# Masks copied by ScalarE, U's products in one group a batch, and small changes of loads, warm-ups and slots

## The chip, the cores and the metric

The kernel runs on one core of one Trainium2 chip. A core has five engines that work side by side: TensorE (PE) multiplies matrices, VectorE (DVE) and ScalarE (ACT) work on elements in the on-chip memory (SBUF) and in the accumulators (PSUM), GpSimd (POOL) works on SBUF, and SyncE (SP) issues transfers. Each engine runs its own list of instructions in order and waits on semaphores of the others. The metric is the device time of one execution in microseconds (us).

## What is computed

Inputs are q, k, v of shape (8, 8, 576, 64), U (576, 32), V (32, 576), w_ch1 (512, 2048) and w_ch2 (2048, 512), all float32. The reference is attention with two kinds of masks, followed by a mixing over the sequence and by an MLP:

```python
rel = pos[:, None] - pos[None, :]
mask_local = (rel >= 0) & (rel < 32)
mask_strided = (rel >= 0) & (pos[None, :] % 32 == pos[:, None] % 32)
# heads 0..3 local, heads 4..7 strided
scores = np.where(masks[None], q @ k.T / 8, -1000000000.0)
attn = np.exp(scores - scores.max(-1))
x = (attn / (attn.sum(-1) + 1e-09)) @ v        # (8, 8, 576, 64), as (8, 576, 512) below
h = x.T @ U @ V
u = x + h.T
out = u + np.maximum(u @ w_ch1, 0.0) @ w_ch2
```

## The kernel before

**The MLP.** The 8 × 576 rows are cut into nine blocks of 512: one for each batch, and a last one (the tail block) with the last 64 rows of all batches. For each block, `gemm1` and `gemm2` run over 16 slices of 128 hidden columns. float32 values are split in a high and a low part: `split` makes uh (ACT, L639) and ul (DVE, L640) of a block, `gemm1` does 12 products of 512 columns into a PSUM tile ph (L648), makes gh = relu(ph) on ACT (L652) and the rest gl on DVE (L653), and `gemm2` does 12 products into the block's accumulators acc (L665): two with gh and one with gl for each of four row groups. `gemm2` runs one slice behind `gemm1`. In the names below gl(w0) is the gl of a block's first slice, gl(w13) that of its fourteenth, ph(w10) the product tile of its eleventh. At the end of a block, `finish` adds acc to the rows on DVE (L672) and stores them. Weights of the first seven slices keep names (w0a, w0b and so on, a for the first layer and b for the second), the others are called w.

**The attention of the following batch** runs beside the MLP. For each batch it has two pairs of local heads (`local_pairs`): scores on PE (L346) on top of a mask that PE writes into the accumulator by a product with the identity (`scores`, L340), maximum and difference on DVE (L356, L357), exp on ACT, transposes on PE (L368), a copy on ACT (L371), the products with v (L381) and the normalising on DVE. All of these use one PSUM tile, px. The four strided heads of batches 2 to 7 (`strided_heads`) take no PE: POOL multiplies (L442 for the scores, L470 for the outputs) and DVE reduces (L444, L472), with softmax steps on DVE and ACT in between (L453 to L461). Reductions run one piece behind products: score row i has one piece up to i = 8 and two from i = 9 on (9 keys and the rest), an output row one piece up to i = 8 and two halves from i = 9 on. The buffers of POOL's pieces come from a group of five that the local pairs and the mixing use too (`att`). Batches 0 and 1 have all their heads done ahead of the MLP, with PE, by `first_attention`.

**The mixing.** `mix_t` multiplies a batch's rows with U in two halves of 256 columns (L514 and, for the last 64 rows, L518), adds the four parts on DVE (L525) and splits the result (L527 to L529); `mix_u` and `mix_tail` multiply it with V (L537, L546) and add it (L539, L552). `transposes` turns the rows (L619) and stores and loads them again as raw.

**What sets the order.** The program is written as a loop over slots, two for each slice. `advance` takes as many steps of the next batch's attention as A_EARLY or A_LATE say for that slot (first slot, last slot, number of steps), `strided_upto` paces the strided heads by S0 and S1, and `issue_after` keeps an instruction behind another. A scheduler then lists the instructions of each engine in the order in which they become ready in its own model of the program's timing, so that a moved slot can change the order on every engine.

**The start.** Masks, an identity in bf16 (both in masks_sb) and one in float32 are loaded on POOL's queue (`far_dma`); ACT's queue (`od_dma`) loads other things. Ahead of the first and of the second group of scores, `scores` runs 8 products of zeros (WARM).

Of the kernel before, what the change touches and what calls it, by code (L numbers as in the profile page):

```python
# [17 lines left out]
NSP = 2  # L18
N_EARLY = 20
N_LATE = 48  # L20
N_STRIDED = 66
# [16 lines left out]
def fused_kernel(ctx, tc, pairs, strided, U, V, w_in, masks, eye, out):  # L38
    nc = tc.nc
    B, S, DM = out.shape  # L40
    D = 64
# [50 lines left out]
    def psx1():  # L92
        return psx2()[:, 0, :]
# [237 lines left out]

    def scores(kT, qT, mask):

        sp = psx2()
        done = marks.setdefault("scores", [])
# [3 lines left out]
        for hh in range(2):  # L339
            nc.tensor.matmul(sp[:, hh, 0:320], ident_b, mask, start=True, stop=False, skip_group_check=True)  # L340
        for c in range(NCH):
            t, c4 = c // 4, c % 4
            k0 = max(0, 32 * c - 32)
            x0 = 64 * t + (0 if c else 32)
            for hh, rows in enumerate(halves):
                last = nc.tensor.matmul(sp[32 * c4:32 * c4 + 32, hh, x0:64 * t + 64], qT[rows, 32 * c:32 * c + 32],  # L346
                                        kT[rows, k0:32 * c + 32], start=False, stop=True, skip_group_check=True,
                                        tile_position=(64 * hh, 32 * c4))
# [25 lines left out]
    def outputs(PT, vt):  # L374

        op = psx2()
        for c in range(NCH):
            t, c4 = c // 4, c % 4
            for o4 in (c4,) if t < 4 else (c4, c4 + 2):
                for hh, rows in enumerate(halves):  # L380
                    last = nc.tensor.matmul(op[32 * o4:32 * o4 + 32, hh, (D + 1) * t:(D + 1) * t + D + 1],  # L381
                                            PT[rows, 32 * c:32 * c + 32], vt[rows, c], start=True, stop=True,
                                            skip_group_check=True, tile_position=(64 * hh, 32 * o4))
        marks.setdefault("PV", []).append(last.ins)
        return op[:, :, 0:5 * (D + 1)].rearrange("p h (t x) -> p h t x", x=D + 1)
# [15 lines left out]
    def local_pairs(b):  # L401
# [100 lines left out]

    def mix_t(b, half):

        xg, xt = x_tiles(b)
        tb = 64 * (b % 2)
        cs = slice(256 * half, 256 * half + 256)
        ps_a = psx1()[:, 0:256]
        if b not in tsts:
            tsts[b] = ap_.tile([96, DM], F32R, name="tst")  # L510
        tst = tsts[b]
        with tc.issue_after(marks["acc"][2 + half]) if b < NSP else nullcontext():
            for j in range(4):
                nc.tensor.matmul(ps_a[32 * j:32 * j + 32, :], U_sb[:, j, :], xg[:, j, cs], start=True, stop=False,  # L514
                                 skip_group_check=True, tile_position=(0, 32 * j))
        for j in range(4):
            part = slice(64 * j, 64 * j + 64)
            nc.tensor.matmul(ps_a[32 * j:32 * j + 32, part], U_sb[tb:tb + 64, 4, :],  # L518
                             xt[tb:tb + 64, 256 * half + 64 * j:256 * half + 64 * j + 64], start=False, stop=True,
                             skip_group_check=True, tile_position=(tb, 32 * j))  # L520
        yield
        ta = att([32, 256], "ta")
        nc.scalar.copy(out=ta, in_=ps_a[0:32, :])  # L523
        for j in range(1, 4):
            nc.vector.tensor_tensor(out=ta, in0=ps_a[32 * j:32 * j + 32, :], in1=ta, op=ALU.add)  # L525
# [44 lines left out]
    def first_attention():  # L570
# [73 lines left out]
    def gemm1(fc, dcs=range(NDC)):  # L644
        ph = ps_h.tile([128, 512], F32, name="ph")
        for dc in dcs:
            for i, (part, ut) in enumerate(((0, uh), (0, ul), (1, uh))):
                nc.tensor.matmul(ph, w_parts[fc, 0][:, part, 128 * dc:128 * dc + 128], ut[:, dc, :],  # L648
                                 start=(dc == dcs[0] and i == 0), stop=(dc == dcs[-1] and i == 2))
        gh = mp.tile([128, 512], F32R, name="gh", bufs=2)  # L650
# [177 lines left out]
```

## Time and profile before

| | us |
|---|---|
| three runs | 1476.99, 928.8, 930.89 |
| median | 930.89 |
| the profiled execution | 928.37 |
| its span | 926.1 |

The profile shows one execution. Its span is the time from the first to the last recorded work; 2.3 us lie around it. By the page PE is busy for 97% of the span, DVE for 59%, POOL for 37% and ACT for 26%. The mean granted clock of PE is 0.991 of full speed. Three views are used below. The timeline lists an engine's instructions with start and duration, neighbours of one kind grouped (x4 is four of them), and in brackets the idle time ahead of them with what ended it. The table by stretch gives busy times. The list of waits gives, for an engine and a line, whom it waited for: total, number, longest. Matmuls are pipelined: their durations overlap, so a matmul's price is the distance from start to start.

### The profile page before, as it was taken

The numbers are of one execution on the slowest core, as the hardware profiler recorded it, in microseconds if no ns is written. First come the engines' busy times: TensorE is split into PE (matmuls) and PEld (weight loads), VectorE is DVE, ScalarE is ACT, GpSimd is POOL, SyncE is SP. The second block draws the span as 40 slices with busy tenths as digits, with TensorE's granted clock in tenths as the row PEclk, the third lists the DMA queues.
The fourth block names the chain that finished last, engine by engine and source line by source line (L and its number), as shares of the span: only waits on it lengthen the run. The fifth ranks groups of instructions, "written<-read, shape, count | busy, mean of one in ns | idle before, by whom it ended". The sixth has DMA issues, their size and how long they took to land.

```text
span 926.1 us, 16819 instructions
## 1 busy us (share of the span) xinstructions
PE 902.6 (97%) x6997; PEld 718.0 (78%) x6998; DVE 548.6 (59%) x895; ACT 244.2 (26%) x478; POOL 338.4 (37%) x378
## 2 busy tenths in 40 slices
PE   7899989999999999999999999999999999999997
PEld 4667767777887788778877787778877888888885
DVE  4579996665886588658765786667863341122111
ACT  3457522142123312331224121422142111121110
POOL 1223493343853393429433764356530000000000
PEclk9899999999999999999999999999999999999999
DMA  9869313201230125011500141014200230001001
GB/s 352 299 205 357 117 54 107 73 2 52 76 145 2 52 55 178 1 52 33 181 8 18 50 168 50 1 53 148 73 1 1 57 120 17 1 1 46 0 1 46
DMA packets 39036, 75.29 MB, mean 81 GB/s; under 512 B 6464, under 2 KB 22864, under 8 KB 37040
## 3 DMA queue, kind: packets, MB, share of 16 engines
q1 hardware_dynamic: 27312, 66.87, 20.7%
q10 hardware_dynamic: 10560, 4.73, 2.0%
q0 software_dynamic: 1088, 2.62, 0.8%
q8 instruction: 55, 0.90, 0.4%
q14 instruction: 21, 0.17, 0.1%
HBM read 54.14 MB, written 11.67 MB: 71 GB/s over the span
## 4 chain that ended last, share of the span: by engine, by line
PE 84%; DVE 4%; DMA 2%; POOL 1%; issue 1%; ACT 0%; SPq 0%; DVEq 0%; ACTq 0%; POOLq 0%
PE acc L665 40%; PE ph L648 39%; PE px L381 1%; DMA w<-in_w_dram 1%; PE px L346 1%; DVE cv L132 1%; DVE s_st L444 1%; PE px L368 1%; PE px L514 1%; DMA od<-x 1%; PE px L537 1%; DMA st<-in_strided_dram 1%; DVE w L206 1%; POOL tmp L442 1%; DVE gl L653 0%
## 5 line engine op out<-in xcount | busy, mean ns | idle before, releaser
L653 DVE SCALAR_TENSOR_TENSOR gl<-ph,gh 128x512 fp32r<-128x512 f32 x144 | 98.9, 688 | 230.1 <-ACT gh L652 229.4
L648 PE MATMUL ph<-uh,w 128*128 128x512 f32 x648 | 215.9, 394 | 0.0
L652 ACT ACTIVATE gh<-ph 128x512 fp32r<-128x512 f32 x144 | 86.2, 599 | 476.9 <-PE ph L648 400.8
L470 POOL TENSOR_TENSOR tmp<-st,s_st 128x448 f32<-128x448 f32 (+7 forms) x162 | 137.3, 876 | 190.8 <-DVE st L472 106.8
L442 POOL TENSOR_TENSOR tmp<-st 128x576 f32<-128x576 f32 (+6 forms) x162 | 175.0, 1121 | 76.5 <-DMA st<-in_strided_dram 66.6
L665 PE MATMUL acc<-w,gh 128*128 128x512 f32 x648 | 196.8, 391 | 0.0
L648 PEld LDWEIGHTS ph<-uh,w 128*128 128x128 f32 x648 | 121.9, 189 | 26.8
L665 PEld LDWEIGHTS acc<-w,gh 128*128 128x128 f32 x648 | 121.3, 188 | 25.6
L472 DVE TENSOR_REDUCE st<-tmp 128x64 f32<-128x64 f32 (+8 forms) x162 | 136.3, 878 | 7.8 <-POOL tmp L470 7.0
L648 PE MATMUL ph<-ul,w 128*128 128x512 f32 x324 | 126.8, 391 | 0.0
L665 PE MATMUL acc<-w,gl 128*128 128x512 f32 x324 | 121.6, 392 | 4.1 <-DVE gl L653 4.1
L444 DVE TENSOR_REDUCE s_st<-tmp 128x9 f32<-128x576 f32 (+6 forms) x162 | 87.2, 563 | 17.5 <-POOL tmp L442 16.7
L665 PEld LDWEIGHTS acc<-w,gl 128*128 128x128 f32 x324 | 61.0, 188 | 18.4 <-DVE gl L653 5.2
L648 PEld LDWEIGHTS ph<-ul,w 128*128 128x128 f32 x324 | 61.1, 189 | 12.6
L487 ACT COPY xg<-st 32x256 f32<-32x256 f32 x96 | 38.8, 404 | 9.1 <-DVE st L472 7.7
L525 DVE TENSOR_TENSOR ta<-px,ta 32x256 f32<-32x256 f32 x42 | 17.6, 420 | 36.5 <-ACT ta L523 35.6
L672 DVE TENSOR_TENSOR xg<-acc,xg 128x512 f32<-128x512 f32 x36 | 22.9, 682 | 13.4 <-PE acc L665 13.4
L539 DVE TENSOR_TENSOR xg<-px,xg 128x512 f32<-128x512 f32 x28 | 18.0, 684 | 11.9 <-PE px L537 11.9
L648 PE MATMUL ph<-uh,w6a 128*128 128x512 f32 x72 | 24.3, 398 | 0.0
L640 DVE TENSOR_TENSOR ul<-raw,uh 128x512 fp32r<-128x512 f32 x32 | 21.1, 682 | 5.3 <-ACT uh L639 5.3
L648 PE MATMUL ph<-uh,w1a 128*128 128x512 f32 x72 | 23.9, 391 | 0.0
L648 PE MATMUL ph<-uh,w2a 128*128 128x512 f32 x72 | 23.9, 391 | 0.0
(265 smaller groups left out, 1252.9 us busy)
## 6 DMA issues: line engine op xcount, KB each, us to landing
w<-in_w_dram SPq DMA_DIRECT2D x9, 1024.0 KB, 13.3
out_dram<-xg SPq DMA_DIRECT2D x32, 256.0 KB, 2.1
v<-in_pairs_dram SPq DMA_DIRECT2D x12, 585.0 KB, 5.1
st<-in_strided_dram SPq DMA_DIRECT2D x6, 1152.0 KB, 5.4
qk<-in_pairs_dram SPq DMA_DIRECT2D x12, 576.0 KB, 5.1
late<-in_pairs_dram SPq DMA_DIRECT2D x8, 585.0 KB, 8.3
late<-in_pairs_dram SPq DMA_DIRECT2D x8, 576.0 KB, 8.1
raw<-bt SPq DMA_DIRECT2D x128, 32.0 KB, 1.9
```

The lines of the kernel that those rows point to most:

```text
L442: nc.gpsimd.tensor_tensor(out=tmp[:, 0:n], in0=sk[:, j0:j0 + n], in1=sq[:, i:i + 1].broadcast_to([128, n, D]), op=ALU.mult)
L444: late.append(lambda tmp=tmp, n=n, i=i, j0=j0: nc.vector.tensor_reduce(out=s_st[:, i, j0:j0 + n], in_=tmp[:, 0:n], axis=AX.X, op=ALU.add))
L470: nc.gpsimd.tensor_tensor(out=tv, in0=sv[:, 0:i + 1, d0:d0 + step], in1=s_st[:, i, 0:i + 1].broadcast_to([128, i + 1, step]), op=ALU.mult)
L472: late.append(lambda tv=tv, i=i, d0=d0, step=step: nc.vector.tensor_reduce(out=o_st[:, i, d0:d0 + step], in_=tv.rearrange("p j d -> p d j" ...
L487: nc.scalar.copy(out=xg[32 * i4:32 * i4 + 32, :, cs], in_=o_st[rows, i4:16:4, :])
L539: nc.vector.tensor_tensor(out=xg[:, t + s, :], in0=pv[:, s, :], in1=xg[:, t + s, :], op=ALU.add)
L640: nc.vector.tensor_tensor(out=lo, in0=raw[:, :, :, dc, :], in1=hi.bitcast(F32), op=ALU.subtract)
L648: nc.tensor.matmul(ph, w_parts[fc, 0][:, part, 128 * dc:128 * dc + 128], ut[:, dc, :], start=(dc == dcs[0] and i == 0), stop=(dc == dcs[-1 ...
L652: marks.setdefault("gh", []).append(nc.scalar.activation(out=gh, in_=ph, func=AF.Relu).ins)
L653: low = nc.vector.scalar_tensor_tensor(out=gl, in0=ph, scalar=0.0, in1=gh.bitcast(F32), op0=ALU.max, op1=ALU.subtract)
L665: last = nc.tensor.matmul(accs[n][s // 2][:, s % 2, :], gt[:, cs], w_parts[fc, 1][:, part, :], start=(fc == 0 and i == 0 and n > 0), stop= ...
L672: nc.vector.tensor_tensor(out=ot, in0=accs[n][s // 2][:, s % 2, :], in1=ot, op=ALU.add)
```

## The change

It has six parts.

- **Masks.** In batches 2 to 7 the mask of a pair is written into px by one ACT copy (`masked`, new) and no longer by two products on PE; the scores then accumulate onto it, and they are issued behind the latest product of gemm1.
- **Outputs.** In `outputs`, only the products of the first of five column groups start a sum afresh; the others add, and are kept behind the first.
- **Mixing.** `mix_t` does all 512 columns at once and stands behind the strided copies; before, its first half stood ahead of them.
- **Loads.** Masks and the identity are loaded on ACT's queue.
- **Warm-ups.** The second group of scores has 3 products of zeros, the first keeps 8.
- **Slots.** A_EARLY has 17 steps for 20, A_LATE has 47 for 48 and begins at slot 3 for 1.

```diff
-N_EARLY = 20
-N_LATE = 48
+N_EARLY = 17
+N_LATE = 47
-A_LATE = (1, 28, N_LATE)
+A_LATE = (3, 28, N_LATE)
-WARM = {0: 8, 1: 8}
+WARM = {0: 8, 1: 3}
...
+    def masked():
+        sp = psx2()
+        nc.scalar.copy(out=sp[:, :, 0:320], in_=mask_l.broadcast_to([128, 320, 2]).rearrange("p x h -> p h x"))
+        return sp
+
+    def scores(kT, qT, mask, sp=None):
+        if sp is None:
+            sp = psx2()
+            with_mask(sp, mask)
...
     def outputs(PT, vt):
         op = psx2()
+        first = None
         for c in range(NCH):
             t, c4 = c // 4, c % 4
+            with tc.issue_after(first) if t else nullcontext():
...
-                                            PT[rows, 32 * c:32 * c + 32], vt[rows, c], start=True, stop=True,
+                                                PT[rows, 32 * c:32 * c + 32], vt[rows, c], start=t == 0, stop=True,
...
-            sp = scores(kT, qT, mask_l)
+            sp = masked()
+            yield
+            with tc.issue_after(marks["ph"][-1]):
+                sp = scores(kT, qT, mask_l, sp)
...
-    def mix_t(b, half):
+    def mix_t(b):
...
-        cs = slice(256 * half, 256 * half + 256)
-        ps_a = psx1()[:, 0:256]
+        ps_a = psx1()
...
-        with tc.issue_after(marks["acc"][2 + half]) if b < NSP else nullcontext():
+        with tc.issue_after(marks["acc"][3]) if b < NSP else nullcontext():
             for j in range(4):
-                nc.tensor.matmul(ps_a[32 * j:32 * j + 32, :], U_sb[:, j, :], xg[:, j, cs], start=True, stop=False,
+                nc.tensor.matmul(ps_a[32 * j:32 * j + 32, :], U_sb[:, j, :], xg[:, j, :], start=True, stop=False,
...
-        ta = att([32, 256], "ta")
+        ta = att([32, 512], "ta")
...
-        far_dma(out=mask_s, in_=masks[:, 448:768])
-        far_dma(out=masks_sb, in_=masks[:, 0:448])
-        far_dma(out=ident, in_=eye)
+        od_dma(out=mask_s, in_=masks[:, 448:768])
+        od_dma(out=masks_sb, in_=masks[:, 0:448])
+        od_dma(out=ident, in_=eye)
...
             yield from local_pairs(b)
-            yield from mix_t(b, 0)
             yield "strided"
             yield from strided_copies(b)
-            yield from mix_t(b, 1)
+            yield from mix_t(b)
```

The order of instructions changes on several engines. In the lists below an instruction stands with its line, operation, output and inputs, and size; the changed kernel's lines are some 11 to 21 higher, and what does the same work keeps its names. L472 before and L493 now are the strided outputs' reductions, L672 and L688 the finishing adds.

On DVE, at the boundary between two batches (the block of batch 2 ends, that of batch 3 begins), from the strided softmax's last multiply on; the first gl is gl(w0). Before:

```order
L461 TENSOR_TENSOR s_st<-s_st,m_st 128x324
L472 TENSOR_REDUCE st<-tmp 128x64 x3
L672 TENSOR_TENSOR xg<-acc,xg 128x512 x2
L472 TENSOR_REDUCE st<-tmp 128x64 x3
L672 TENSOR_TENSOR xg<-acc,xg 128x512 x2
L653 SCALAR_TENSOR_TENSOR gl<-ph,gh 128x512 x2
```

Now, from the third and fourth ul on:

```order
L482 TENSOR_TENSOR s_st<-s_st,m_st 128x324
L655 TENSOR_TENSOR ul<-raw,uh 128x512 x2
L493 TENSOR_REDUCE st<-tmp 128x64 x4
L688 TENSOR_TENSOR xg<-acc,xg 128x512 x2
L493 TENSOR_REDUCE st<-tmp 128x64 x2
L688 TENSOR_TENSOR xg<-acc,xg 128x512 x2
L493 TENSOR_REDUCE st<-tmp 128x64 x3
L669 SCALAR_TENSOR_TENSOR gl<-ph,gh 128x512
```

Nine reductions stand ahead of gl(w0), where six stood. At the five boundaries from batch 1 to 2 up to batch 5 to 6 the counts are 10, 9, 11, 9 and 9 now, and 6 at each before.

On PE at the same boundary, from the scores of the pair to the first products with gl(w0). Before:

```order
L648 MATMUL ph<-uh,w1a 128x512
L346 MATMUL px<-qk 32x32 x2
L346 MATMUL px<-qk 32x64 x34
L665 MATMUL acc<-w0b,gh 128x512 x2
L665 MATMUL acc<-w0b,gl 128x512
L665 MATMUL acc<-w0b,gh 128x512 x2
```

Now, where the last product of the second slice's gemm1 is directly ahead of these:

```order
L663 MATMUL ph<-uh,w1a 128x512
L681 MATMUL acc<-w0b,gh 128x512 x4
L681 MATMUL acc<-w0b,gl 128x512
L681 MATMUL acc<-w0b,gh 128x512 x2
L681 MATMUL acc<-w0b,gl 128x512 x2
L681 MATMUL acc<-w0b,gh 128x512 x2
```

The scores now stand behind the second slice's gemm2, and four products with gh stand ahead of the first with gl. In all, from the start of the fifteenth slice's gemm2 to that first product with gl there are now 52 products of 512 columns and nothing else.

On DVE, some 20 us ahead of the boundary, where the strided scores are reduced (L444 before, L465 now); the gl shown is gl(w13). Before:

```order
L444 TENSOR_REDUCE s_st<-tmp 128x9
L444 TENSOR_REDUCE s_st<-tmp 128x6
L552 TENSOR_TENSOR xt<-px,xt 64x512
L444 TENSOR_REDUCE s_st<-tmp 128x9
L444 TENSOR_REDUCE s_st<-tmp 128x7
L653 SCALAR_TENSOR_TENSOR gl<-ph,gh 128x512
```

Now:

```order
L465 TENSOR_REDUCE s_st<-tmp 128x6
L465 TENSOR_REDUCE s_st<-tmp 128x9
L569 TENSOR_TENSOR xt<-px,xt 64x512
L465 TENSOR_REDUCE s_st<-tmp 128x7
L465 TENSOR_REDUCE s_st<-tmp 128x9
L669 SCALAR_TENSOR_TENSOR gl<-ph,gh 128x512
L465 TENSOR_REDUCE s_st<-tmp 128x8
```

One more reduction of nine keys stands ahead of gl(w13). The first of these reductions stood ahead of gl(w10) before, between the adds of the second half of `mix_t` (L525); now it stands behind gl(w10) and the first add of the whole `mix_t` (L542), whose products stand on PE directly behind ph(w10).

On ACT, the mask copy of a batch's first pair stands directly ahead of the four uh casts at the boundary. The scores of batch 2's first pair, which stood in five groups of 20, 8, 10, 6 and 28 instructions among the products, are one group now.

More of the change, by code (lines that the diff above doesn't have):

```diff
@@ L330, in od_reads, with with_mask @@
             far_dma(out=xt[tb + 32 * i4:tb + 32 * i4 + 32, 256:512], in_=ov[16 + i4])
-    def scores(kT, qT, mask):
-        sp = psx2()
+    def with_mask(sp, mask):
         done = marks.setdefault("scores", [])
@@ L340, in scores @@
             nc.tensor.matmul(sp[:, hh, 0:320], ident_b, mask, start=True, stop=False, skip_group_check=True)
+    def masked():
[6 more added lines that the diff above has]
+            with_mask(sp, mask)
+        done = marks.setdefault("scores", [])
         for c in range(NCH):
@@ L376, in outputs @@
         op = psx2()
+        first = None
         for c in range(NCH):
             t, c4 = c // 4, c % 4
[L379 to L383 removed]
+            with tc.issue_after(first) if t else nullcontext():
+                for o4 in (c4,) if t < 4 else (c4, c4 + 2):
+                    for hh, rows in enumerate(halves):
+                        last = nc.tensor.matmul(op[32 * o4:32 * o4 + 32, hh, (D + 1) * t:(D + 1) * t + D + 1],
+                                                PT[rows, 32 * c:32 * c + 32], vt[rows, c], start=t == 0, stop=True,
+                                                skip_group_check=True, tile_position=(64 * hh, 32 * o4))
+            if t == 0:
+                first = last.ins
         marks.setdefault("PV", []).append(last.ins)
@@ L501, in x_tiles @@
         return xgs[b], tails[b // 2]
-    def mix_t(b, half):
+    def mix_t(b):
         xg, xt = x_tiles(b)
         tb = 64 * (b % 2)
-        cs = slice(256 * half, 256 * half + 256)
-        ps_a = psx1()[:, 0:256]
-        if b not in tsts:
-            tsts[b] = ap_.tile([96, DM], F32R, name="tst")
-        tst = tsts[b]
-        with tc.issue_after(marks["acc"][2 + half]) if b < NSP else nullcontext():
+        ps_a = psx1()
+        tst = tsts[b] = ap_.tile([96, DM], F32R, name="tst")
+        with tc.issue_after(marks["acc"][3]) if b < NSP else nullcontext():
             for j in range(4):
-                nc.tensor.matmul(ps_a[32 * j:32 * j + 32, :], U_sb[:, j, :], xg[:, j, cs], start=True, stop=False,
+                nc.tensor.matmul(ps_a[32 * j:32 * j + 32, :], U_sb[:, j, :], xg[:, j, :], start=True, stop=False,
                                  skip_group_check=True, tile_position=(0, 32 * j))
         for j in range(4):
[L517 to L520, printed above, removed]
+            part = slice(128 * j, 128 * j + 128)
+            nc.tensor.matmul(ps_a[32 * j:32 * j + 32, part], U_sb[tb:tb + 64, 4, :], xt[tb:tb + 64, part],
+                             start=False, stop=True, skip_group_check=True, tile_position=(tb, 32 * j))
         yield
-        ta = att([32, 256], "ta")
+        ta = att([32, 512], "ta")
         nc.scalar.copy(out=ta, in_=ps_a[0:32, :])
@@ L526, in mix_t @@
         yield
-        nc.scalar.copy(out=tst[0:32, cs], in_=ta)
-        nc.scalar.copy(out=tst[64:96, cs], in_=ta)
-        nc.vector.tensor_tensor(out=tst[32:64, cs], in0=ta, in1=tst[0:32, cs].bitcast(F32), op=ALU.subtract)
+        nc.scalar.copy(out=tst[0:32], in_=ta)
+        nc.scalar.copy(out=tst[64:96], in_=ta)
+        nc.vector.tensor_tensor(out=tst[32:64], in0=ta, in1=tst[0:32].bitcast(F32), op=ALU.subtract)
         yield
@@ L607, in attention @@
             yield from mix_tail(0)
-            for half in range(2):
-                yield from mix_t(b, half)
+            yield from mix_t(b)
             yield from mix_u(b)
@@ L647, in gemm1 @@
             for i, (part, ut) in enumerate(((0, uh), (0, ul), (1, uh))):
-                nc.tensor.matmul(ph, w_parts[fc, 0][:, part, 128 * dc:128 * dc + 128], ut[:, dc, :],
-                                 start=(dc == dcs[0] and i == 0), stop=(dc == dcs[-1] and i == 2))
+                last = nc.tensor.matmul(ph, w_parts[fc, 0][:, part, 128 * dc:128 * dc + 128], ut[:, dc, :],
+                                        start=(dc == dcs[0] and i == 0), stop=(dc == dcs[-1] and i == 2))
+        marks.setdefault("ph", []).append(last.ins)
         gh = mp.tile([128, 512], F32R, name="gh", bufs=2)
```

## The prediction

> **What bounds the kernel now.** I read the page's shares first, then busy time by stretch, the list of waits, and last the timelines of PE, DVE, ACT and POOL around the places that the change touches. The chain of work that ended last is four fifths PE's two large products, and by stretch PE is busy without a gap from 139 us on, while DVE, the next engine, has more than a quarter to spare:
>
> ```profile
> PE acc L665 40%; PE ph L648 39%; PE px L381 1%; DMA w<-in_w_dram 1%; PE px L346 1%; DVE cv L132 1%; DVE s_st L444 1%; PE px L368 1%; PE px L514 1%; DMA od<-x 1%; PE px L537 1%; DMA st<-in_strided_dram 1%; DVE w L206 1%; POOL tmp L442 1%; DVE gl L653 0%
> ```
> ```profile
> 120.00:139.00 19.00, 15.23 (x57) 11.06 (x55) 18.91 (x25) 4.32 (x7) 17.30 (x13) 0.91 0.23 67
> ...
> 236.00:333.00 97.00, 97.00 (x740) 77.40 (x739) 69.47 (x116) 25.44 (x55) 52.13 (x58) 1.00 0.20 66
> ```
> Columns are, after the stretch and its length, the busy time of PE, PEld, DVE, ACT and POOL. Before 139 us (19.00 us with 18.91 on DVE) DVE sets the pace; behind it PE does, so a microsecond of PE work saved is a microsecond of span, and so is a microsecond in which PE waits. The list of waits shows how little PE waits for DVE's split of the hidden layer (gl) today, three times in the whole span:
>
> ```profile
> PE acc L665 <- DVE gl L653: 4.1, 3, 1.9
> ```
> That small sum is a matter of timing, not of spare room. The batch boundary at 351 us shows it, first on PE (start, duration):
>
> ```profile
> 351.06 1.07 PE L665 MATMUL acc<-w,gh 128*128 128x512 f32 x4
> 351.97 0.39 PE L665 MATMUL acc<-w,gl 128*128 128x512 f32 x1
> ...
> 361.71 0.39 PE L648 MATMUL ph<-uh,w1a 128*128 128x512 f32 x1
> 362.03 0.92 PE L346 MATMUL px<-qk 64*32 64x32 f32 x72
> 362.88 0.73 PE L665 MATMUL acc<-w0b,gh 128*128 128x512 f32 x2
> 363.45 0.39 PE L665 MATMUL acc<-w0b,gl 128*128 128x512 f32 x1
> ```
> Four matmuls take 351.97 − 351.06 = 0.91 us, so one takes 0.227 and a step of 24 takes 5.44. The first second-layer product of the new batch that needs gl(w0) starts at 363.45; the pair's scores (72 rows from 362.03) stand ahead of it. On DVE and ACT at the same place:
>
> ```profile
> 351.89 0.69 DVE L653 SCALAR_TENSOR_TENSOR gl<-ph,gh 128x512 fp32r<-128x512 f32 x1 [1.69 <-ACT gh L652]
> ...
> 355.49 0.48 DVE L461 TENSOR_TENSOR s_st<-s_st,m_st 128x324 f32<-128x324 f32 x1
> 356.44 0.65 DVE L472 TENSOR_REDUCE st<-tmp 128x64 f32<-128x64 f32 x2 [0.46 <-POOL tmp L470]
> 357.27 0.38 DVE L472 TENSOR_REDUCE st<-tmp 128x64 f32<-128x192 f32 x1 [0.17 <-POOL tmp L470]
> 357.56 1.28 DVE L672 TENSOR_TENSOR xg<-acc,xg 128x512 f32<-128x512 f32 x2
> 358.76 2.01 DVE L472 TENSOR_REDUCE st<-tmp 128x64 f32<-128x256 f32 x3
> 360.69 1.27 DVE L672 TENSOR_TENSOR xg<-acc,xg 128x512 f32<-128x512 f32 x2
> 361.88 0.68 DVE L653 SCALAR_TENSOR_TENSOR gl<-ph,gh 128x512 fp32r<-128x512 f32 x1
> ...
> 364.97 3.08 DVE L472 TENSOR_REDUCE st<-tmp 128x64 f32<-128x448 f32 x3
> ```
> ```profile
> 352.12 2.17 ACT L639 CAST uh<-raw 128x512 fp32r<-128x512 f32 x4
> ```
> gl(w0) ends at 361.88 + 0.68 = 362.56, which is 0.9 us ahead of its need. From 355.49 on DVE hardly rests (0.46 and 0.17 us) ahead of it: six strided reductions (2 + 1 + 3) and four finishing adds. The next three reductions stand behind it and take 3.08.
>
> **The change, part by part. Masks of batches 2 to 7.** Twelve times two mask matmuls leave PE. What one pair of them costs is read where it stands alone between products:
>
> ```profile
> 442.66 0.45 PE L340 MATMUL px<-masks_sb 128*128 128x320 bf16 x2
> 442.83 1.19 PE L665 MATMUL acc<-w,gh 128*128 128x512 f32 x4
> 443.86 0.39 PE L665 MATMUL acc<-w,gl 128*128 128x512 f32 x1
> ```
> ```profile
> L371 ACT COPY PT<-px 128x576 f32<-128x576 f32 x12 | 7.7, 641 | 20.5 <-PE px L368 20.5
> ```
> Without the two, the fifth product would start at 442.66 + 4 × 0.227 = 443.57 instead of 443.86: 0.29 us each, 12 × 0.29 = 3.5 us gained. In their place stands an ACT copy of 640 columns; the nearest row, ACT's copy of 576, takes 0.641, so 12 × 0.7 on an engine that is busy 25.44 of 97 us. One copy a batch is queued ahead of the four uh casts (2.17 us at 352.12), and DVE's ul waits for those. By the new order DVE does its normalising multiply (355.49) between two ul, so it stays busy, and I take 0; without that cover it is 0.64 × 5 = 3.2, the upper end. A copy also waits until px, the one tile that it writes, has been read: at the boundary that is the last add of the mixing, long done; for the second pair it is DVE's normalising of the first, and behind the copy stand only the gh of a step whose ph comes later. The second copy ends some 3 us ahead of its scores by the new order and costs nothing.
>
> **U's products in one group.** One half of the old form:
>
> ```profile
> 415.58 0.39 PE L665 MATMUL acc<-w,gl 128*128 128x512 f32 x1
> 415.90 0.64 PE L514 MATMUL px<-xg,U_sb 128*32 128x256 f32 x8
> 416.47 0.32 PE L518 MATMUL px<-xt,U_sb 64*32 64x64 f32 x8
> 416.71 0.50 PE L648 MATMUL ph<-uh,w 128*128 128x512 f32 x1
> 417.05 0.39 PE L648 MATMUL ph<-ul,w 128*128 128x512 f32 x1
> ```
> The matmul at 417.05 would have started at 415.58 + 2 × 0.227 = 416.04, so one half costs 1.01 us of PE, two cost 2.02. Of this 0.57 is the wide products, 0.24 the small ones, 0.20 the way in and out. If the group costs by its columns, it takes 0.20 + 1.14 + 0.48 = 1.82 and saves 0.2; if its small half costs by instructions, it saves up to 0.5. I take 0.35, the middle, times six batches: 2.1 us. In the stretch that DVE bounds, its adds shrink as well:
>
> ```profile
> L525 DVE TENSOR_TENSOR ta<-px,ta 32x256 f32<-32x256 f32 x42 | 17.6, 420 | 36.5 <-ACT ta L523 35.6
> L539 DVE TENSOR_TENSOR xg<-px,xg 128x512 f32<-128x512 f32 x28 | 18.0, 684 | 11.9 <-PE px L537 11.9
> ```
> Six of 0.420 become three that cost at most what 512 columns on four times the partitions do (0.684): 2.52 − 2.05 = 0.5 us once. That the strided outputs' later matmuls lose their start flag changes no count or size of an instruction: 0.
>
> **Scores in one piece.** Before, batch 2's first pair stood in five pieces among products; each way in and out costs the 0.20 just read, and four fewer are 0.8 us. The ordering behind ph delays no other scores that PE or DVE was waiting for.
>
> **The start.** PE's first real work waited for the masks, and the second warm-up group follows:
>
> ```profile
> 7.75 0.45 PE L340 MATMUL acc<-early,masks_sb 128*128 128x320 bf16 x2 [2.89 <-DMA masks_sb<-in_masks_dram]
> 9.37 3.16 PE L338 MATMUL px<-raw 128*128 128x512 bf16 x7 [0.33 <-issue]
> ```
> ```profile
> 4.00:29.00 25.00, 17.30 (x485) 10.92 (x483) 12.28 (x22) 10.84 (x22) 2.94 (x6) 0.93 1.02 397
> ```
> Masks on the other queue could give back at most the 2.89 us waited at 7.75, and five fewer warm-ups at most 5 × 3.16 / 7 = 2.3. But from 4 to 29 us the DMA share is 1.02 (last column but one): all 16 engines are loading what the following work needs, so an earlier start is met by the same arrivals. The loads that were ahead on ACT's queue move back by three issues, which could cost as much. I take 0 for both, with −2 to +2 for the range. At half clock a matmul takes 3.16 / 7 = 0.45, twice 0.227. The Trainium skill, TensorE: Matmul & The Clock Gate, section "What's actually happening", has the full clock granted only after a window of about 3.4 us with PE busy, so that three warm-ups might not open it. The trace agrees as far as it goes, with seven slow ones in 3.16 us and full speed behind them; by that rule the scores behind the warm-ups would run slow and the sum would be some 1 us higher.
>
> The gains are 3.5 + 2.1 + 0.5 + 0.8 = 6.9 us.
>
> **What the new order costs.** It comes from moved slots, and two gl are placed worse. First, gl(w0) at five boundaries (batches 1→2 to 5→6). DVE now does 10, 9, 11, 9 and 9 strided reductions ahead of it, instead of 6. Three more are the 3.08 us seen at 364.97: gl(w0) ends at 362.56 + 3.0 = 365.5. PE asks for it earlier than before, since the scores now stand behind: from 351.06 there are 23 of the old products, 24 of the new ones, 1 left over and 4 that need only gh, 52 × 0.227 = 11.8, so at 362.85. PE waits 365.5 − 362.85 = 2.6 us. Five of these are 13 us; the boundaries with 10 and 11 have one and two more half reductions of about 3.08 / 3 × 320 / 512 = 0.64, together 2. Nothing in this order gives the time back: behind the wait PE has its full 24 a step to do.
>
> Second, gl(w13). POOL's products for the strided scores follow each other without a gap, since DVE's reductions free its few buffers:
>
> ```profile
> 417.72 0.20 DVE L444 TENSOR_REDUCE s_st<-tmp 128x1 f32<-128x64 f32 x1
> ...
> 440.20 0.68 DVE L653 SCALAR_TENSOR_TENSOR gl<-ph,gh 128x512 fp32r<-128x512 f32 x1
> ```
> ```profile
> 418.00 16.26 POOL L442 TENSOR_TENSOR tmp<-st 128x256 f32<-128x256 f32 x16 [1.51 <-DVE s_st L444]
> 434.71 10.34 POOL L442 TENSOR_TENSOR tmp<-st 128x576 f32<-128x576 f32 x8 [0.45 <-DVE s_st L444]
> ```
> ```profile
> 419.34 0.39 PE L648 MATMUL ph<-uh,w 128*128 128x512 f32 x1
> ```
> Let P be the end of ph(w10), 419.34 + 0.23 = 419.57. POOL ran from 418.00 (P − 1.6), let go by DVE's first reduction at 417.72, to 434.71 + 10.34 = 445.05. In the new order the first reduction stands behind U's products (1.6 us behind P), ACT's copy (0.6) and a DVE add (0.7), so POOL is let go near P + 3.2, 4.8 us later. gl(w13), done at 440.88 before, now stands behind one more wide reduction, whose product POOL ended 4.1 us (three of the last) before 445.05, at P + 21.4; now P + 25.7 to 26.2, and with the reduction and gl itself P + 27.1 to 27.6. PE asks for it after U's 1.6 us, 100 products (22.7) and V's 1.1: P + 25.4. The wait is up to 2.2 us. Its start is a sum of three estimates and gains 2.5 us if POOL starts as early as before, which leaves none: between 0 and 2.2 I take 1.0, five times, 5 us, since the page calls POOL's spans rough.
>
> **Sum:** 928.4 (the profiled execution: span 926.1 and 2.3 around it) − 6.9 + 13 + 2 + 5 = 941.5; I say 941. The median of the runs, 930.9, lies 2.5 above the profiled one, the lowest 0.4; I add nothing.
>
> **The rivals.** *Gains alone.* DVE keeps up, because POOL and DVE get ahead while the pairs begin two slots later, and neither gl is late. For it speaks that PE waited only 4.1 us for gl in the whole span; against it the row counts ahead of gl(w0). It gives 928.4 − 6.9 = 921.5. *One wait only.* gl(w0) alone gives 936.5, gl(w13) at 1 to 2 us alone 926.5 to 931.5. *Slower: POOL later still.* The load that the strided outputs need is issued when POOL has done its last score product:
>
> ```profile
> DMA to landing us min/median/max: 3.8/4.7/6.1
> ```
> If POOL is let go 1.9 us later than I take it, which the upper end of the sum above comes near (1.2), gl(w13) is 1.9 us later in five batches and the time is 941 + 9.5 = 950.5. From about 1.7 us on it decides; with the load landing after 6.1 us, the outputs start late too and it needs less. Against it: POOL's first three products are done ahead. *The change does less than it says* is the gains' lower end: with 0.2 for U and 0 for the start, 0.9 us less.
>
> **How the numbers follow.** Both waits near my figures: 0.33, 937 to 947. One wait: 0.25, 926 to 937. Gains alone: 0.25, 917 to 925 with the start's ±2. POOL later: 0.17, 949.5 and more. The likeliest gives 941. From 919 to 951 about a fifth is left out, 0.06 below and 0.13 above. A measurement tells 2% from no change, which is 912.3 and 949.5 about the median: 0.02 faster (gains alone, with a start that gives back all it waited and more), 0.17 slower, 0.81 the same.
>
> **What would show it.** Masks: no mask matmul behind the start, 12 ACT copies near 0.7. U: one group a batch of 1.5 to 1.9 us. The waits: PE for gl at 13 to 25 us in the list, in ten places or more, and stretches of 97 us that take longer by 3 us with PE idle. If PE's wait for gl stays under 5 us, the row counts misled me, and the time is near 921; if the first part of the span, up to 139 us, moves by more than 2 us, my sum for the start is wrong.

## The result and the profile after

The changed kernel takes 958.48 us (median of 4 runs, 955.49 to 960.02), the kernel before 929.85 beside it: a ratio of 1.031, with a 95% interval of 1.027 to 1.035. One of the four runs of the kernel before took 1476.99 us and is left out of the ratio. The change is slower, and above the range of 919 to 951. The profiled execution took 955.49 us with a span of 953.7; its mean granted clock is 0.982, where it was 0.991.

The list of waits of the changed kernel (total, number, longest) has PE waiting for gl, as the prediction spoke of, and for L688, the finishing add, which frees the accumulators. From 139 us on the two come to 24.3 us, near the 15 and the up to 11 that its worked-out figures gave:

```profile
PE acc L681 <- DVE gl L669: 19.7, 12, 2.9
PE acc L681 <- DVE xg L688: 7.9, 3, 3.6
```

The busy time by stretch has a column that did not move before, the granted clock, third from the end:

```profile
139.00:236.00 97.00, 97.00 (x725) 77.88 (x724) 64.82 (x101) 25.90 (x53) 46.64 (x51) 1.00 0.15 52
236.00:333.00 97.00, 92.07 (x692) 72.66 (x691) 61.80 (x99) 25.72 (x53) 45.50 (x49) 0.98 0.19 62
333.00:430.00 97.00, 92.38 (x686) 72.96 (x685) 60.83 (x100) 24.54 (x52) 44.12 (x49) 0.96 0.21 68
430.00:527.00 97.00, 91.73 (x675) 73.23 (x674) 63.91 (x101) 25.11 (x52) 49.70 (x53) 0.96 0.20 66
```

From 236 us on PE now loses 5 us of each 97, and besides the clock falls to 0.96 and 0.98, where the kernel before has 1.00 in all of these. PE's timeline around one boundary shows how the two hang together (start, duration, and the idle time ahead with its end):

```profile
347.41 0.50 PE L681 MATMUL acc<-w,gl 128*128 128x512 f32 x1 [1.90 <-DVE gl L669]
...
350.06 0.63 PE L663 MATMUL ph<-uh,w 128*128 128x512 f32 x1
350.49 0.63 PE L663 MATMUL ph<-ul,w 128*128 128x512 f32 x1
...
353.49 0.39 PE L663 MATMUL ph<-uh,w 128*128 128x512 f32 x1
...
364.60 1.21 PE L681 MATMUL acc<-w0b,gh 128*128 128x512 f32 x4
368.54 0.50 PE L681 MATMUL acc<-w0b,gl 128*128 128x512 f32 x1 [2.73 <-DVE gl L669]
...
370.41 1.05 PE L681 MATMUL acc<-w0b,gh 128*128 128x512 f32 x2
371.26 0.63 PE L681 MATMUL acc<-w0b,gl 128*128 128x512 f32 x1
...
372.98 0.39 PE L663 MATMUL ph<-ul,w2a 128*128 128x512 f32 x1
```

At 347.41 PE has waited 1.90 us for gl(w13), at 368.54 2.73 us for gl(w0). Behind each, a product's start is 0.43 us from the next (350.06 to 350.49) where it is 0.227 otherwise: half speed. The stretches, cut at these places, say the same in the clock column:

```profile
338.00:345.00 7.00, 7.00 (x32) 5.74 (x31) 5.77 (x10) 0.60 (x1) 7.00 (x7) 1.00 0.29 71
348.00:352.00 4.00, 4.00 (x12) 3.12 (x11) 2.94 (x5) 0.00 (x0) 1.71 (x2) 0.57 0.24 55
353.00:364.00 11.00, 11.00 (x50) 9.09 (x49) 8.58 (x18) 4.26 (x8) 5.91 (x9) 1.00 0.62 250
368.60:372.00 3.40, 3.40 (x9) 2.71 (x10) 1.75 (x3) 0.00 (x0) 1.72 (x3) 0.57 0.00 0
```

From the first product with w3a of one block to that of the next the whole difference can be laid out. Starts in us, from the two timelines:

| block | 0 | 1 | 2 | 3 | 4 | 5 | 6 |
|---|---|---|---|---|---|---|---|
| before | 67.04 | 177.43 | 274.77 | 372.06 | 469.39 | 566.67 | 664.01 |
| after | 65.16 | 170.23 | 273.65 | 378.48 | 483.77 | 586.98 | 691.64 |

At block 1 the changed kernel is 7.2 us ahead. Over the next five blocks it loses 34.8 (521.41 against 486.58), and behind that nothing (262.06 to the end of the span against 262.09): 34.8 − 7.2 = 27.6, the difference of the spans. In these five blocks PE waits 24.3 us for DVE, in twelve places. The clock is at half for 27.3 us, added up from the granted clock in the trace; 1.4 us of these are waits, and the other 25.9 cost half of their length, 13.0. That is 37.3, less 2.5 us, which is what is left of the gains in these blocks.

### The profile page after: what moved, and what is told of

It reads as the page before. It is cut to its first block, busy times and chain, and to the rows that moved or that the text cites. A ratio compares the mean times of both kernels' runs of the same rounds, so it can differ in the third digit from the quotient of the medians.

```text
span 953.7 us, 16491 instructions
## 1 busy us (share of the span) xinstructions
PE 907.0 (95%) x6857; PEld 720.2 (76%) x6857; DVE 545.0 (57%) x867; ACT 249.0 (26%) x469; POOL 343.1 (36%) x375
## 4 chain that ended last, share of the span: by engine, by line
PE 76%; DVE 10%; POOL 2%; DMA 1%; SPq 1%; issue 1%; ACT 0%; DVEq 0%; POOLq 0%; ACTq 0%
PE acc L681 36%; PE ph L663 35%; DVE st L493 2%; POOL tmp L491 2%; DVE xg L688 1%; PE px L397 1%; DVE s_st L465 1%; SPq L96 1%; PE px L357 1%; DMA st<-in_strided_dram 1%; DVE gl L669 1%; PE px L379 1%; DVE cv L132 1%; PE px L532 1%; DVE w L206 1%
## 5 line engine op out<-in xcount | busy, mean ns | idle before, releaser
L669 DVE SCALAR_TENSOR_TENSOR gl<-ph,gh 128x512 fp32r<-128x512 f32 x144 | 98.8, 687 | 296.0 <-ACT gh L668 295.5
L463 POOL TENSOR_TENSOR tmp<-st 128x576 f32<-128x576 f32 (+6 forms) x162 | 177.2, 1132 | 92.1 <-DVE s_st L465 50.1
L491 POOL TENSOR_TENSOR tmp<-st,s_st 128x448 f32<-128x448 f32 (+7 forms) x162 | 141.7, 903 | 188.9 <-DVE st L493 130.2
L663 PEld LDWEIGHTS ph<-uh,w 128*128 128x128 f32 x648 | 122.2, 189 | 25.9
L493 DVE TENSOR_REDUCE st<-tmp 128x64 f32<-128x64 f32 (+8 forms) x162 | 136.2, 875 | 3.7 <-POOL tmp L491 3.2
L465 DVE TENSOR_REDUCE s_st<-tmp 128x9 f32<-128x576 f32 (+6 forms) x162 | 86.8, 561 | 15.5 <-POOL tmp L463 14.5
L663 PEld LDWEIGHTS ph<-ul,w 128*128 128x128 f32 x324 | 61.1, 189 | 12.9
L681 PE MATMUL acc<-w0b,gh 128*128 128x512 f32 x72 | 26.7, 466 | 7.9 <-DVE xg L688 7.9
L688 DVE TENSOR_TENSOR xg<-acc,xg 128x512 f32<-128x512 f32 x36 | 22.9, 682 | 11.1 <-PE acc L681 11.1
L655 DVE TENSOR_TENSOR ul<-raw,uh 128x512 fp32r<-128x512 f32 x32 | 23.1, 742 | 5.2 <-ACT uh L654 3.4
L681 PEld LDWEIGHTS acc<-w0b,gh 128*128 128x128 f32 x72 | 15.8, 225 | 12.5 <-DVE xg L688 9.5
L681 PE MATMUL acc<-w0b,gl 128*128 128x512 f32 x36 | 17.6, 527 | 7.7 <-DVE gl L669 7.7
L663 PE MATMUL ph<-uh,w5a 128*128 128x512 f32 x72 | 24.5, 401 | 0.0
```

Of the source, the lines that this page charges most:

```text
L463: nc.gpsimd.tensor_tensor(out=tmp[:, 0:n], in0=sk[:, j0:j0 + n], in1=sq[:, i:i + 1].broadcast_to([128, n, D]), op=ALU.mult)
L465: late.append(lambda tmp=tmp, n=n, i=i, j0=j0: nc.vector.tensor_reduce(out=s_st[:, i, j0:j0 + n], in_=tmp[:, 0:n], axis=AX.X, op=ALU.add))
L491: nc.gpsimd.tensor_tensor(out=tv, in0=sv[:, 0:i + 1, d0:d0 + step], in1=s_st[:, i, 0:i + 1].broadcast_to([128, i + 1, step]), op=ALU.mult)
L493: late.append(lambda tv=tv, i=i, d0=d0, step=step: nc.vector.tensor_reduce(out=o_st[:, i, d0:d0 + step], in_=tv.rearrange("p j d -> p d j" ...
L655: nc.vector.tensor_tensor(out=lo, in0=raw[:, :, :, dc, :], in1=hi.bitcast(F32), op=ALU.subtract)
L663: last = nc.tensor.matmul(ph, w_parts[fc, 0][:, part, 128 * dc:128 * dc + 128], ut[:, dc, :], start=(dc == dcs[0] and i == 0), stop=(dc == ...
```

## The experiments

I had two theories for the clock. Theory A: PE standing idle brings it down. Rival B: something else in these places does. Beside that stood the question which part of the change moves the reductions.

**e1, e2 and e3: gl put ahead of the reductions by hand.** The edit of e1, with O_FREE = 6 (e2 does the same for the scores' reductions and gl(w13), e3 both, and gl(w14) too):

```diff
-                late.append(lambda tv=tv, i=i, d0=d0, step=step: nc.vector.tensor_reduce(
-                    out=o_st[:, i, d0:d0 + step], in_=tv.rearrange("p j d -> p d j"), axis=AX.X, op=ALU.add))
+                def total(tv=tv, i=i, d0=d0, step=step):
+                    with tc.issue_after(marks["gl"][NFC * (b - 1)]) if i >= O_FREE else nullcontext():
+                        nc.vector.tensor_reduce(out=o_st[:, i, d0:d0 + step], in_=tv.rearrange("p j d -> p d j"), axis=AX.X,
+                                                op=ALU.add)
+                late.append(total)
```

> The changed kernel with one thing more: from row 7 on, the strided outputs' reductions on DVE are issued behind gl(w0), so that at most six stand ahead of it. Nothing is left out. Theory A (the reductions ahead of gl(w0) make PE wait, and each wait of some 2 us or more is followed by a stretch at half clock that costs some 1.7 us more): the five waits at the boundaries (15.6 us in all) and about six of the eight stretches at half clock (10 us) go, so about 25 us less than the changed kernel, near 934. Rival B (the clock falls for another reason, such as a load limit, and stays down as often): only the 15.6 us, near 943. Rival C (PE only moves its wait to the next gl, or to the load for the strided outputs): under 8 us gained.

> The changed kernel with one thing more: the strided scores' reductions from the second piece of row 16 on are issued behind gl(w13), as in the kernel before. Nothing is left out. Theory A: the waits for gl(w13) (8.6 us in five places) become some 0.3 us each, but gl(w14) then stands behind the whole rest of the reductions and the softmax's two steps and waits about 1.3 us in its place: 1 to 3 us gained, 956 to 958. Rival C (gl(w14) has room enough): 7 us and two or three half-clock stretches, 11 us gained, near 947.

> The changed kernel with gl(w0), gl(w13) and gl(w14) each put ahead of DVE's reductions (of row 7 on, of row 16's second piece on, of row 18 on). Nothing is left out. Theory A: no wait of PE for DVE over 1 us between 139 and 690 us, no half clock there, and what the change gains is left: 918 to 924. Rival B (half clock for another reason): 930 to 937. Rival D (the change's gains are smaller than I worked out, or the masks' copies on ACT delay uh): 925 to 931.

Measured: e1 932.21 us (1.0036 of the kernel before, 1.0022 to 1.0051), e2 950.0 (1.0241, 1.0209 to 1.0273), e3 922.15 (0.9928, 0.9904 to 0.9951). e1 came down by 26 us where the waits alone are 15.6, so the clock went with them, as theory A has it; one stretch at half clock is left between 139 and 690 us, behind a wait for gl(w13). In e3 none is left. In e2, gl(w14) took over less than I expected:

```profile
448.15 0.50 PE L684 MATMUL acc<-w,gl 128*128 128x512 f32 x1 [0.43 <-DVE gl L672]
454.41 0.50 PE L684 MATMUL acc<-w,gl 128*128 128x512 f32 x1 [0.52 <-DVE gl L672]
468.61 1.22 PE L684 MATMUL acc<-w0b,gh 128*128 128x512 f32 x2 [3.46 <-DVE xg L691]
```

0.43 us for gl(w13), 0.52 for gl(w14), which has more room than my 1.3, and 3.46 us at the boundary, which the edit leaves alone. e3 is faster than both kernels of this case.

**e5 and e6: which part moves the reductions.** e5 puts one number back (shown). e6 puts the mixing back in two halves, with 20 and 50 steps in the slots for 17 and 47, since the halves are more steps:

```diff
-A_LATE = (3, 28, N_LATE)
+A_LATE = (1, 28, N_LATE)
```

> The changed kernel with one number put back: A_LATE begins at slot 1 as before, not at 3. Nothing is left out. DVE's order then has 7, 6, 6 and 6 strided reductions ahead of gl(w0) at the boundaries from batch 2 on, as the kernel before has, and the order around gl(w13) stays as in the changed kernel. Theory A (the later slots cause the waits for gl(w0), the mixing in one group behind the copies causes those for gl(w13)): gl(w0) waits under 1 us, gl(w13) still 1.6 to 1.9 in five places, near 933. Rival E (the slots do not matter, the masks' copies or the scores behind ph cause the waits): no nearer than 950.

> The changed kernel with the mixing put back into two halves, the first ahead of the strided copies. Nothing is left out. gl(w13) then stands ahead of row 16's reductions as before, 9 or 10 strided reductions still stand ahead of gl(w0). Theory A: no wait for gl(w13) over 0.6 us, the waits for gl(w0) stay near 15 us with their half clock, two more us of products: 948 to 953. Rival E: gl(w13) waits as in the changed kernel, near 960.

Measured: e5 920.58 us (0.9918, 0.9891 to 0.9944), e6 955.89 (1.0301, 1.0276 to 1.0325). e5 did more than either theory expected: both waits are gone, not only those for gl(w0). From 139 us on PE waits for nothing. The reason for gl(w13) is on PE, not on DVE. In e5 POOL is let go 3.03 us behind the start of U's products and gl(w13) ends 27.7 us behind it (311.29, 314.32, 338.95), nearly as in the changed kernel (319.93, 322.96, 347.36). But U's products stand one gemm1 earlier in PE's list, ahead of ph(w10) and not behind it, so PE asks 28.15 us behind their start, where it asked after 25.6.

In e6 the wait for gl(w13) is at most 0.1 us, gl(w14) waits 0.3 to 0.6, and the boundary costs as much as before it; the waiting product there is the one that needs freed accumulators. The first row is for gl(w14):

```profile
358.13 0.50 PE L687 MATMUL acc<-w,gl 128*128 128x512 f32 x1 [0.28 <-DVE gl L675]
371.72 1.22 PE L687 MATMUL acc<-w0b,gh 128*128 128x512 f32 x2 [2.83 <-DVE xg L694]
```

**e10: the same number in the kernel before.**

```diff
-A_LATE = (1, 28, N_LATE)
+A_LATE = (3, 28, N_LATE)
```

> The kernel before with one number changed: A_LATE begins at slot 3, not 1. Nothing is left out. DVE's order then has 8 strided reductions ahead of gl(w0) at most boundaries, 6 before, and gl(w13) stands where it stood. Theory A: PE waits some 1 to 2 us for gl(w0) at four or five boundaries, too short for half clock, and not for gl(w13): 934 to 940. Rival G (the later slots alone make the whole loss): over 950. Rival H (they cost nothing without the other parts): 929.

Measured: 943.17 us (1.0166, 1.015 to 1.0183), 3 us over what I expected of theory A and far from rival G. As expected, PE does not wait for gl(w13), and no stretch at half clock lies between 139 and 690 us. The waits at the boundary are of the expected size at the first one alone; the first row here is for gl(w14):

```profile
256.87 0.50 PE L665 MATMUL acc<-w,gl 128*128 128x512 f32 x1 [0.28 <-DVE gl L653]
...
269.16 0.74 PE L665 MATMUL acc<-w0b,gh 128*128 128x512 f32 x2 [0.82 <-DVE xg L672]
270.85 0.50 PE L665 MATMUL acc<-w0b,gl 128*128 128x512 f32 x1 [0.68 <-DVE gl L653]
```

0.28 + 0.82 + 0.68 us here, 0.8 to 1.0 us at each of the other four boundaries: 5.5 us in all. The five blocks take 12.9 us more than before (2.1 to 3.5 each), so 7.4 are no listed wait. The scores' products, which stand in more pieces, make up a part of these: from start to start they take 2.11 to 2.33 us a block, where they took 1.70; the rest is open. So the later slots cost the kernel before about half of what the changed one loses, and less than half of that is waits. In e6, which has the same first slots and the old mixing, the loss is nearly whole: the waits at the boundary are 2.7 to 3.5 us, and each is followed by half clock (371 to 378 us behind the one shown), which e10's shorter ones are not.

**e4 and e9: PE's idle time and the clock, alone.** e4 delays DVE by hand in the last two blocks, which have no attention; e9 fills four of the eight waits:

```diff
+        for _ in range(PLAN.get((n, fc), 0)):
+            low = nc.vector.tensor_reduce(out=spare, in_=ph.rearrange("p (a x) -> p a x", x=64), axis=AX.X, op=ALU.add)
...
+                if i == 2 and s == 0 and (n, fc) in FILL:
+                    for _ in range(FILL[n, fc]):
+                        with tc.issue_after(last.ins):
+                            last = nc.tensor.matmul(accs[n][0][:, 0, 0:448], nought, masks_sb, start=False, stop=False,
+                                                    skip_group_check=True)
```

> The kernel before with eight delays of DVE in the last two blocks, where no attention runs: 9, 11, 13, 15 and 10, 12, 14, 16 extra reductions of ph stand ahead of one gl each, three slices apart, so that PE waits from about 0.3 to 5 us. The extra sums are not used. Theory A: waits up to some 1.5 us cost their length, longer ones also leave PE at half clock for about 3.4 us, which costs 1.7 us more each; in sum some 20 us of waits and 8 to 10 us of clock. Rival B: the clock stays at 1.00 in all eight and the time grows by the waits alone.

> The kernel of e4_gaps with four of its eight waits (2.8, 4.2, 3.5 and 4.9 us there) filled: 13, 20, 17 and 24 products of zeros run on PE ahead of the product that waits. They add zeros to the sum. Theory A (half clock comes from PE standing idle): the clock stays at 1.00 behind the four filled waits and falls as before behind the waits of 5.7 and 6.4 us that are not filled; the time is 11 to 12 us less than e4_gaps's, near 975. Rival F (half clock comes from something else that goes with these places): the same clock at all, near 986.

Measured: 986.22 us for e4, 980.05 for e9, one run each. In e4 PE waited 1.40, 1.86, 2.78, 3.51, 4.18, 4.91, 5.68 and 6.41 us. That is 30.7 in all, more than the 20 I gave, since an extra reduction takes 0.72 us. The stretches right behind the waits of 1.40, 2.78, 4.18, 5.68 and 1.86 us (in this order of rows; the granted clock is third from the end):

```profile
774.00:778.00 4.00, 3.94 (x17) 3.23 (x18) 0.60 (x2) 0.00 (x0) 0.00 (x0) 1.00 0.32 70
794.00:797.40 3.40, 3.40 (x9) 2.64 (x9) 0.32 (x1) 0.00 (x0) 0.00 (x0) 0.51 0.00 0
816.50:823.00 6.50, 6.50 (x19) 5.12 (x20) 0.51 (x1) 0.00 (x0) 0.00 (x0) 0.63 0.01 3
841.30:845.00 3.70, 3.70 (x9) 2.92 (x10) 0.55 (x1) 0.00 (x0) 0.00 (x0) 0.50 0.00 0
884.00:888.00 4.00, 3.93 (x17) 3.22 (x18) 0.61 (x2) 0.00 (x0) 0.00 (x0) 1.00 0.01 4
```

In this run, waits of 1.40 and 1.86 us leave the clock at 1.00. Behind the one of 2.78 us it is at half for 3.4 us, and with those of 3.51 us and more for 6.8, of which 1.2 to 3.5 us still lie in the wait. In e9 the stretches behind the filled waits of 2.78, 4.18, 3.51 and 4.91 us, with the unfilled one of 5.68 as the third row:

```profile
795.50:799.00 3.50, 3.50 (x15) 2.87 (x16) 0.52 (x1) 0.00 (x0) 0.00 (x0) 1.00 0.00 0
816.70:823.00 6.30, 6.30 (x28) 5.12 (x29) 1.16 (x2) 0.60 (x1) 0.00 (x0) 1.00 0.00 1
839.30:843.00 3.70, 3.70 (x9) 2.93 (x10) 0.48 (x1) 0.00 (x0) 0.00 (x0) 0.50 0.00 0
902.60:909.00 6.40, 6.40 (x28) 5.26 (x29) 1.18 (x2) 0.60 (x1) 0.00 (x0) 1.00 0.01 3
924.40:931.00 6.60, 6.60 (x29) 5.37 (x30) 1.22 (x2) 0.60 (x1) 0.00 (x0) 1.00 0.00 0
```

The products of zeros took the place of idle time, 0.3 to 0.4 us of wait was left, and the clock stayed at 1.00, while it fell behind both waits that were not filled. That rules rival F out for these four places. From block 7 to block 8 (the starts with w3a, 770.47 to 876.35 against 768.77 to 878.31 in e4) e9 is 3.7 us shorter; the whole time differs by 6.2 and not the 11 to 12 I gave. e9 had lost 1.7 us ahead of these blocks, and I had counted the long stretches of e4 whole, though 1.9, 1.2 and 1.8 us of the three lie in the wait, where half clock costs nothing: 9.5 us for the four places. The last 1.6 us stay open.

**e7, e8, e11 and e12: what the parts are worth.** e7 is e3 with the masks on PE, e8 the kernel before with the loads and warm-ups alone, e12 is e5 again, and e11 is e12 with the mixing in halves (and 20 and 50 steps). The edit of e7 against e3:

```diff
-            sp = masked()
-            yield
-            with tc.issue_after(marks["ph"][-1]):
-                sp = scores(kT, qT, mask_l, sp)
+            sp = scores(kT, qT, mask_l)
```

> The kernel of e3_all with one part of the change undone: the masks of batches 2 to 7 are written by PE again, and the scores are not tied to ph. Nothing is left out. Against e3_all's 922: the theory (0.29 us a pair, and 0.8 us of scores in pieces) says 3.5 to 4.3 us more, 925.5 to 926.5. Rival (the copies on ACT give back what PE saves): 922 as e3_all.

> The kernel before with two parts of the change alone: masks and identity loaded on ACT's queue, and three warm-ups ahead of the second scores. Nothing is left out. The theory (the engines' loads hold the start anyway): within 2 us of the kernel before, 927 to 931. Rival (PE's start is what counts, 2.9 us waited and 2.3 us of warm-ups): 924 to 926.

> The kernel of e5_slots (slot 1) with the mixing in two halves again. Nothing is left out. By the two kernels' traces a group costs 1.54 us and two halves 2.02: 6 times 0.48, so 2.9 us more than e5_slots in the same call. If the group's place matters more than its price, it differs by another sum.

> The kernel of e5_slots once more, with more rounds and beside e11_slots_halves: 0.989 to 0.994 of the kernel before, 919 to 923.

Measured: e7 926.95 us (0.9982, 0.9966 to 0.9997), 4.8 over e3; e8 928.27 (0.9997, 0.9981 to 1.0013), no difference; e12 921.5 (0.9915, 0.9895 to 0.9935); e11 928.59 (1.0004, 0.9991 to 1.0018), 7.1 over e12 and not 2.9. e11's order has a wait of its own in one batch (1.64 us at 253.95), and its stretch ahead of 139 us, which DVE bounds, is longer: from block 0 to block 1 it takes 109.7 us, e12 106.0, with one stretch at half clock at 129 us that e12 does not have. That stretch can account for up to 1.7 of the 3.7 us. In the four blocks behind, which PE bounds and in which neither kernel waits, e11 takes 0.1 to 0.6 us longer than e12, 0.4 in the mean, close to the 0.48 of the two prices. So what goes beyond my 2.9 us lies in the stretch that DVE bounds and in that one wait.

A busy PE with the clock at 1.00, as e12 has it in the stretches in which the changed kernel lost 5 us each:

```profile
236.00:333.00 97.00, 97.00 (x722) 77.55 (x721) 68.65 (x111) 26.30 (x54) 52.35 (x57) 1.00 0.20 66
333.00:430.00 97.00, 97.00 (x720) 77.33 (x719) 68.30 (x110) 26.32 (x54) 51.88 (x56) 1.00 0.21 68
```

## Why the prediction was wrong

**The waits at the five boundaries: right in place and in sum.** I gave 2.6 us each and 2 more, 15 in all; measured 15.6. This is DVE of the changed kernel at the boundary of the prediction:

```profile
361.14 1.28 DVE L688 TENSOR_TENSOR xg<-acc,xg 128x512 f32<-128x512 f32 x2
362.34 1.49 DVE L493 TENSOR_REDUCE st<-tmp 128x64 f32<-128x320 f32 x2
363.74 1.28 DVE L688 TENSOR_TENSOR xg<-acc,xg 128x512 f32<-128x512 f32 x2
364.94 2.95 DVE L493 TENSOR_REDUCE st<-tmp 128x64 f32<-128x448 f32 x3
367.80 0.68 DVE L669 SCALAR_TENSOR_TENSOR gl<-ph,gh 128x512 fp32r<-128x512 f32 x1
```

Finishing adds and reductions follow each other without a gap up to gl(w0), the three extra ones last (2.95 us, 3.08 in the kernel before). At three boundaries PE waits for the finishing add first (3.04, 3.65 and 1.25 us), ahead of which some of the same reductions stand; 7.9 of the 15.6 us are such waits. The prediction had none of these: at these three its sum is right, but PE waits for another instruction than it named.

**gl(w13): right in place, too small in size.** I worked out up to 2.2 us and took 1.0, on the ground that its start was a sum of estimates. It measured 1.62, 1.90, 1.62, 1.90 and 1.62: 8.7 in all against 5. PE, POOL and DVE there, the first row being the end of ph(w10):

```profile
319.61 0.39 PE L663 MATMUL ph<-uh,w 128*128 128x512 f32 x1
```
```profile
322.96 22.76 POOL L463 TENSOR_TENSOR tmp<-st 128x256 f32<-128x256 f32 x21 [10.01 <-DVE s_st L465]
```
```profile
345.35 1.28 DVE L465 TENSOR_REDUCE s_st<-tmp 128x7 f32<-128x448 f32 x2
346.67 0.69 DVE L669 SCALAR_TENSOR_TENSOR gl<-ph,gh 128x512 fp32r<-128x512 f32 x1
```

POOL is let go at 322.96, 3.1 us behind P (319.61 + 0.23 = 319.84), where I had 3.2, and its pieces follow without a gap as they did before. gl(w13) ends at 347.36, P + 27.5, where I had 27.1 to 27.6. There was no reason to halve the wait. The rival "POOL later still" gives a time over 949.5 too, but not by what happened: POOL was not later than I took it.

**The step that failed is the price of a wait.** The prediction says: "Nothing in this order gives the time back: behind the wait PE has its full 24 a step to do." It counted those 24 at full clock. Six of the waits (or pairs of them, at the boundaries) were followed by stretches at half clock, two of them of double length, and these cost 13.0 us that no term of the sum held. With 15.6 for 15 and 8.7 for 5 alone the sum would have been 945.8, inside the range; with 13.0 for nothing it is 928.4 − 6.9 + 15.6 + 8.7 + 13.0 = 958.8, against the profiled 955.5 (the gains in the two spans came to 7.2 + 2.5 = 9.7 and not 6.9). I used the clock for the warm-ups alone, where it made no difference (e8), and did not ask what the waits that I forecast would do to it.

The trace of the kernel before had an example, in the row 120 to 139 us that the prediction shows with a clock of 0.91. Its longest wait for gl is followed by 3.4 us at half clock:

```profile
130.39 0.50 PE L665 MATMUL acc<-w,gl 128*128 128x512 f32 x1 [1.90 <-DVE gl L653]
```
```profile
131.90:135.20 3.30, 3.30 (x9) 2.61 (x8) 3.24 (x5) 0.00 (x0) 3.30 (x4) 0.50 0.21 79
```

The Trainium skill, TensorE: Matmul & The Clock Gate, section "HAM oscillation — how this bites in real kernels", says that PE should have no idle gaps over some 3.4 us. By that figure only the wait of 3.65 us would have counted among those of the changed kernel; here 1.90 us was enough at 347.41 and was not at 557.53, 1.86 us in e4 was not, and 2.7 us and more was enough each time in these two traces. The measurement decides.

**The gains: right in sum, not in parts.** e12 gains 7.9 us (0.0085 × 928.5) where I gave 6.9, but the blocks that PE bounds take 96.9 us (five from 173.24 to 657.70) for 97.3, where 0.93 less was worked out. A part of the difference is in the scores: their products take 1.84 to 2.05 us a block there from start to start, 1.70 in the kernel before. What I called 0.5 us for the stretch from block 0 to block 1 is about 4 (106.0 us in e12, 110.4 before). Up to 1.7 of it is the half clock of the kernel before at 131.9 us, which e12 does not have; the rest is open. The changed kernel gains there as well, 5.3 of its 7.2 us up to block 1, so the prediction's sign for this (more than 2 us up to 139 us) came true, and its sum for that part is wrong. The group of the mixing costs what its lower price gave; in e5:

```profile
310.97 0.39 PE L681 MATMUL acc<-w,gl 128*128 128x512 f32 x1
311.29 1.06 PE L532 MATMUL px<-xg,U_sb 128*32 128x512 f32 x8
312.28 0.42 PE L536 MATMUL px<-xt,U_sb 64*32 64x128 f32 x8
312.64 0.50 PE L663 MATMUL ph<-uh,w 128*128 128x512 f32 x1
312.97 0.39 PE L663 MATMUL ph<-ul,w 128*128 128x512 f32 x1
```

From 311.20, when the next product would have started, to 312.97 less one product's 0.227 are 1.54 us, against 2.02 for two halves: 0.48, where I had 0.35 and "up to 0.5". The masks are worth 4.8 us by e7 and e3 (their intervals leave some 2.5 either way), 4.3 by my count with the scores in one piece. The start is worth nothing, as I took it.

**Which part did it.** I wrote that the waits come "from moved slots" without saying which part moved them. One number does, A_LATE's first slot (e5). In the kernel before it costs half as much, and no half clock (e10), so the whole loss needs it together with other parts of the change. Everything else in the change is together a gain of 0.85% (e12).

## What to carry to other kernels

Where PE is the bound, price a wait of PE for its length and for the clock behind it: here a wait of 1.9 us sometimes, and one of 2.6 us or more nearly always, was followed by 3.4 or 6.8 us at half clock. The half clock costs half of what it lasts behind the wait, so 1.7 to 3.4 us on top. A change that saves work on the bounding engine but shifts the pacing of the work beside it must be read in the order of the other engines: count what stands ahead of the instruction that the bounding engine waits for. And try a pacing number at its old value before giving up the rest; here that one number was the difference between 3% slower and 0.8% faster.

## What was not expected of the hardware

The clock's fall has steps, and the length of the wait is not all that sets them. Over all traces of this case, from 100 us on, no wait of PE of up to 1.64 us that stands alone was followed by half clock. Of 13 such waits of 1.86 to 1.91 us 8 were, and of 22 from 2.61 us on all but one (2.61 us at 571.50 in e2). With 3.51 us and more it always lasted 6.8 us; but 3.46 us in e2 brought 3.4 and 2.83 us in e6 brought 6.8. In each trace the changes of the granted clock lie whole multiples of 3.413 us apart (in the changed kernel stretches of 3.41, 6.83, 17.07, 81.92 and 98.99 us). So the place of a wait on this grid seems to count beside its length: the wait at 347.41 lies between two of these points, that at 557.53, as long and without half clock, has one in its middle, at 556.80. Moving a wait on the grid was not tried.

The distance from product to product in `gemm1` is not the same in all kernels, away from any edit. In e4 a block without a delay takes 98.8 us (376.11 to 474.88 from w3a to w3a) where the kernel before takes 97.3, at a granted clock of 1.00 and without waits. Its products in `gemm1` start 0.234 us apart in the median of such a block, those in `gemm2` 0.230; in the kernel before and in e12 both are 0.227. e9 shows the same as e4, on another chip. Both hold added tiles in the on-chip memory. Whether the place of the tiles does it was not tried.
